# A start-up and a schedule changed at once: load order, word conversion, warm-up length and the order of the late products in a fused attention and expert kernel

## The chip, the cores and the metric

The kernel runs on one core of one Trainium2 chip. The metric is the device time of one execution in microseconds (us), the smaller the better.

## The reference

The reference is an attention block whose keys and queries go through a polynomial sketch, followed by four experts. It is cut here to what the argument needs.

```python
def _attn_ref(q, k, v, S1, S2):            # q, k, v: (4, 4, 1088, 32), S1 and S2: (8, 32)
    def phi(x):
        a = np.einsum('rd,bhsd->bhsr', S1, x)
        b = np.einsum('rd,bhsd->bhsr', S2, x)
        return np.einsum('bhsi,bhsj->bhsij', a, b).reshape(*x.shape[:-1], r * r)
    q_p, k_p = phi(q), phi(k)
    kv = np.einsum('bhsf,bhsd->bhfd', k_p, v)
    z = np.sum(k_p, axis=2)
    num = np.einsum('bhsf,bhfd->bhsd', q_p, kv)
    den = np.einsum('bhsf,bhf->bhs', q_p, z)[..., None] + 1e-06
    return num / den
# ... x is the attention's output, 4352 tokens by 128; then for four experts
#     out += p[:, e] * (relu(x @ w1[e]) @ w2[e])        # w1: 128 x 1024, w2: 1024 x 128
```

S1 and S2 arrive as 64-bit floats. The kernel reads them as pairs of 32-bit words and makes 32-bit floats of them with integer operations.

## The kernel before

Nothing can be projected until S and the first batch of k are on the chip. The start-up therefore is a race: S's two loads, word operations on VectorE and a transpose on one side, k's load and its transpose on the other. TensorE meanwhile runs matmuls on zeros to get its clock up: in the profile below the full clock is granted from 4.33.

```python
s_raw = cpool.tile([R2, 2 * D], I32, name="s_raw")
for i, (eng, src) in enumerate(((nc.scalar, S1), (nc.sync, S2))):
    eng.dma_start(s_raw[R * i : R * i + R, :], src.bitcast(I32))
# ...
load_rows(k, 0, "kn")                     # 128 rows of 4352 bytes, on SyncE
load_rows(q, 0, "qn", slice(0, P))
vn[0] = load_v(0)
# ...
keep_warm(10)                             # 128x128x512 bf16 matmuls on zeros
# ...
bits(s_f[:, hi], high, 1, shl, 21, shr)   # first of 14 word operations
# ...
nc.vector.tensor_tensor(out=s_hl[0:R2, :], in0=s_n[:, :], in1=s_f[:, :].bitcast(F32), op=ALU.mult)
nc.vector.transpose(s_T[:, :], s_hl[:, :])
for h in range(H):                        # weights of the key projection
    nc.scalar.copy(_ap(sk, ...), _ap(s_T, ...))
for i in range(3):
    nc.gpsimd.tensor_copy(_ap(sp, ...), _ap(s_T, ...))
for h in range(H):                        # weights of the query projection
    nc.gpsimd.tensor_copy(_ap(sr, ...), _ap(sp, ...))
# ...
def start():                              # in this order: transposes of k and q, key projection (h<-sk,kT),
    ...                                   # query projection (o<-qT,sr), sums over keys (f<-vx,kp),
                                          # den and num of the first 128 tokens, division, first expert
```

The later units of tokens are cut into pieces that are dealt out between the expert matmuls. `yield` ends a piece; the schedule counts 19 pieces a unit. A late piece is the product of queries with the summed keys (den<-kvx,qp on TensorE), which needs two products made by VectorE, p = 0 and p = 1.

```python
            for p in range(2):
                query_product(qp, p, x, n, qa, qb)
                yield
        yield
        yield
        yield from (attend_first if b == 0 and c < START[2] else attend)(b, c, n, qp)
# ... in attend():
            for t in range(T[0]):
                for p in range(2):
                    for _ in range(2):
                        on_side(...)      # one den<-kvx,qp matmul
# ... in attend_first():
        nc.vector.transpose(dT[:, 0:n], nd[0][:, 0:n])
        nc.vector.tensor_scalar(out=rc, in0=_ap(dT, ...), scalar1=1e-6, ...)   # den + 1e-6
        nc.vector.reciprocal(rc, rc)
```

## Time and profile before

| quantity | before |
|---|---|
| time, median of 4 runs | 491.62 us (491.28 to 491.96) |
| span of the profiled run, granted clock | 489.5 us, 0.999 |
| S landed, k landed | 2.37, 4.94 us |
| first key matmul | 5.82 us |
| clock granted in full from | 4.33 us |
| first expert matmul, last matmul starts | 14.16, 485.88 us |

The table's first line has one run more than the three that the prediction speaks of.

### The profile page before, as it was taken

How to read it: one execution, taken by the hardware profiler on the slowest of the kernel's cores; microseconds unless marked ns; L12 is line 12 of the kernel's file. 1: busy time of each engine (PE TensorE's matmuls, PEld its weight loads, DVE VectorE, ACT ScalarE, POOL GpSimd, SP SyncE). 2: the span in 40 equal slices, each digit the busy share in tenths (PEclk: the TensorE clock that was granted, in tenths of full speed). 3: DMA queues.
4: the chain of work that ended last, by engine and by line, in shares of the span. 5: the costliest groups of instructions: out<-in, count | busy, mean ns of one | idle time of the engine just before them, and what ended most of it. 6: DMA issues, size and time to landing. Idle time of an engine off the chain costs nothing.

```text
span 489.5 us, 11439 instructions
## 1 busy us (share of the span) xinstructions
PE 482.6 (99%) x4602; PEld 361.1 (74%) x4602; DVE 318.5 (65%) x746; ACT 244.4 (50%) x487; POOL 226.8 (46%) x260
## 2 busy tenths in 40 slices
PE   8999999999999999999999999999999999999997
PEld 5877777777767777555777777777777777878997
DVE  6759585868676757768675564575575666665642
ACT  3344463455445634535455464445455455566651
POOL 6052473516355444334555353444555355555570
PEclk9999999999999999999999999999999999999999
DMA  7990230040102520041102200031101200120000
GB/s 207 290 284 22 88 95 1 2 137 1 34 2 80 139 55 1 1 118 23 33 2 87 50 0 1 2 87 23 33 1 55 49 1 1 50 50 2 15 3 18
DMA packets 37588, 26.25 MB, mean 54 GB/s; under 512 B 26016, under 2 KB 34592, under 8 KB 37024
## 3 DMA queue, kind: packets, MB, share of 16 engines
q1 hardware_dynamic: 37520, 25.53, 19.0%
q8 instruction: 36, 0.59, 0.5%
q14 instruction: 16, 0.13, 0.1%
q10 hardware_dynamic: 16, 0.00, 0.0%
HBM read 21.28 MB, written 4.24 MB: 52 GB/s over the span
## 4 chain that ended last, share of the span: by engine, by line
PE 96%; DVE 2%; DMA 1%; issue 0%; ACT 0%; SPq 0%; DVEq 0%
PE h L188 49%; PE o L188 40%; PE f L188 4%; PE den L188 3%; DMA kn<-in_k_dram 1%; DVE qp L450 1%; DVE hid L698 1%; PE num L188 1%; PE h L176 0%; DVE kT L314 0%; ACT hid L723 0%; DVE qa L584 0%; ACT sh L842 0%; SPq L119 0%; DVE xT L486 0%
## 5 line engine op out<-in xcount | busy, mean ns | idle before, releaser
L188 PE MATMUL h<-xT,w_sb 128*64 128x512 f32 (+4 forms) x1408 | 300.2, 495 | 0.5 <-DVE xT L486 0.5
L698 DVE SCALAR_TENSOR_TENSOR hid<-h,hid 128x256 f32<-128x256 f32 (+6 forms) x432 | 203.6, 472 | 148.2 <-ACT hid L723 139.2
L723 ACT ACTIVATE hid<-h 128x512 f32<-128x512 f32 (+3 forms) x288 | 158.4, 550 | 195.0 <-PE h L188 157.0
L188 PE MATMUL o<-hid,w2s 128*64 128x256 f32 (+3 forms) x1152 | 221.6, 355 | 0.0
L188 PE MATMUL o<-hid,w_sb 128*64 128x256 f32 (+3 forms) x864 | 183.9, 355 | 0.0
L188 PEld LDWEIGHTS h<-xT,w_sb 128*64 128x64 f32 x1408 | 144.2, 137 | 51.8 <-issue 9.2
L188 PEld LDWEIGHTS o<-hid,w2s 128*64 128x64 f32 x1152 | 131.7, 137 | 30.9 <-issue 0.2
L838 POOL TENSOR_TENSOR ev<-yz,sh 64x256 f32<-64x256 f32 (+3 forms) x72 | 48.4, 672 | 163.5 <-ACT sh L841 160.8
L188 PEld LDWEIGHTS o<-hid,w_sb 128*64 128x64 f32 x864 | 101.0, 137 | 24.5 <-issue 6.3
L826 POOL TENSOR_TENSOR yz<-ev 128x512 f32<-128x512 f32 (+3 forms) x36 | 42.1, 1170 | 61.8 <-ACT ev L829 61.8
L838 POOL TENSOR_TENSOR ct<-ev 128x512 f32<-128x512 f32 (+3 forms) x36 | 42.0, 1167 | 2.8
L838 POOL TENSOR_TENSOR ct<-ct,gate 128x512 f32<-128x512 f32 (+3 forms) x27 | 32.1, 1189 | 2.1
L838 POOL TENSOR_TENSOR total<-total,ct 128x512 f32<-128x512 f32 (+3 forms) x27 | 31.8, 1179 | 2.1
L450 DVE TENSOR_TENSOR qp<-qa,qb 64x384 f32<-64x384 f32 (+3 forms) x44 | 32.1, 729 | 1.0
L828 ACT COPY ev<-o 128x512 f32<-128x512 f32 (+3 forms) x36 | 19.4, 539 | 11.3 <-PE o L188 10.8
L188 PE MATMUL o<-w_sb,hid 128*64 128x128 f32 x256 | 21.7, 273 | 0.0
L829 ACT COPY ev<-o 128x512 f32<-128x512 f32 (+3 forms) x36 | 19.4, 539 | 2.6
L715 ACT ACTIVATE hid<-h 128x256 f32<-128x256 f32 x24 | 9.2, 384 | 21.2 <-PE h L188 20.7
L188 PEld LDWEIGHTS o<-w_sb,hid 128*64 128x64 f32 x256 | 17.8, 137 | 2.1 <-issue 1.9
L353 DVE TENSOR_TENSOR kp<-fs 128x256 f32<-128x256 f32 (+1 forms) x24 | 14.7, 617 | 0.0
L841 ACT COPY sh<-yz 64x256 f32<-64x256 f32 (+3 forms) x36 | 13.7, 379 | 1.7 <-POOL yz L826 0.8
L842 ACT COPY sh<-yz 64x256 f32<-64x256 f32 (+3 forms) x36 | 13.7, 380 | 0.9
(113 smaller groups left out, 230.2 us busy)
## 6 DMA issues: line engine op xcount, KB each, us to landing
w_sb<-in_moe_w_dram SPq DMA_DIRECT2D x8, 512.0 KB, 7.5
gate<-gates SPq DMA_DIRECT2D x4, 1024.0 KB, 5.5
kn<-in_k_dram SPq DMA_DIRECT2D x4, 544.0 KB, 4.6
vn<-in_v_dram SPq DMA_DIRECT2D x16, 128.0 KB, 4.2
gate<-gates SPq DMA_DIRECT2D x2, 896.0 KB, 5.7
qn<-in_q_dram SPq DMA_DIRECT2D x3, 544.0 KB, 5.5
xd<-y SPq DMA_DIRECT2D x26, 48.0 KB, 1.7
out_dram<-ob SPq DMA_DIRECT2D x16, 64.0 KB, 2.0
```

The source lines that it names most:

```text
L188: nc.tensor.matmul(out(s), weights(s), moving(s), **flags)
L353: eng.tensor_tensor(out=_ap(kps[b], 0, P, 256 * t0 + P * p + 64 * x, [[256, n], [32, 2], [R, 4], [1, R]]), in0=_ap(src, 0, P, off + 4 * x, ...
L450: nc.vector.tensor_tensor(out=qp[p][64 * x : 64 * x + 64, 0:n], in0=qa[64 * p : 64 * p + 64, 0:n], in1=qb[64 * p : 64 * p + 64, 0:n], op=A ...
L698: nc.vector.scalar_tensor_tensor(out=out, in0=src, scalar=0.0, in1=in1, op0=ALU.max, op1=ALU.subtract)
L715: nc.scalar.activation(hd[:, 0 : 2 * n], hp[:, 0 : 2 * n], ACTF.Relu)
L723: nc.scalar.activation(hd[:, n * j : n * j + n], hp[:, 0:n], ACTF.Relu)
L826: add = lambda out, in0, in1, op=ALU.add: nc.gpsimd.tensor_tensor(out=out, in0=in0, in1=in1, op=op)
L828: nc.scalar.copy(_ap(ev, 0, P, 0, [[2 * w, 2], [1, w]]), _ap(a0, 0, P, 0, two))
L829: nc.scalar.copy(_ap(ev, 0, P, w, [[2 * w, 2], [1, w]]), _ap(a1, 0, P, 0, two))
L838: add = lambda out, in0, in1, op=ALU.add: nc.gpsimd.tensor_tensor(out=out, in0=in0, in1=in1, op=op)
L841: nc.scalar.copy(sh[HP:P, 0:w], yz[0:HP, 0, 0:w])
L842: nc.scalar.copy(sh[0:HP, 0:w], yz[HP:P, 1, 0:w])
```

## The change

The intent is to start the real work sooner and to remove a wait in the middle. k's load goes first in SyncE's queue, and both S loads go into ScalarE's. The words take 12 operations instead of 14. The copies of S are shared by ScalarE and GpSimd. The warm-up loses two matmuls. The 1e-6 of the first unit's denominator is added by matmuls. The late products run pair by pair (all tokens of p = 0, then all of p = 1), and a unit gets a 20th, empty piece before them.

```diff
     s_raw = cpool.tile([R2, 2 * D], I32, name="s_raw")
-    for i, (eng, src) in enumerate(((nc.scalar, S1), (nc.sync, S2))):
-        eng.dma_start(s_raw[R * i : R * i + R, :], src.bitcast(I32))
+    load_rows(k, 0, "kn")
+    for i, src in enumerate((S1, S2)):
+        nc.scalar.dma_start(s_raw[R * i : R * i + R, :], src.bitcast(I32))
...
-    load_rows(k, 0, "kn")
     load_rows(q, 0, "qn", slice(0, P))
...
-    keep_warm(10)
+    keep_warm(8)
...
-    def either(out, a, b):
-        nc.vector.tensor_tensor(out=out, in0=a, in1=b, op=ALU.bitwise_or)
+    def either(out, in0, s1, op0, in1):
+        nc.vector.scalar_tensor_tensor(out=out, in0=in0, scalar=s1, in1=in1, op0=op0, op1=ALU.bitwise_or)
...
-    bits(s_x[:, lo], low, 29, shr)
-    either(s_x[:, hi], s_x[:, hi], s_x[:, lo])
+    either(s_x[:, hi], low, 29, shr, s_x[:, hi])
-    bits(s_e[:, :], s_f[:, :], 23, shl)
-    either(s_f[:, :], s_e[:, :], s_m[:, :])
+    either(s_f[:, :], s_f[:, :], 23, shl, s_m[:, :])
...
+    def copy_on(scalar):
+        return nc.scalar.copy if scalar else nc.gpsimd.tensor_copy
     for h in range(H):
-        nc.scalar.copy(...)                      # sk
+        copy_on(h < 2)(...)                      # sk: two on ScalarE, two on GpSimd
...                                              # sp and sr are shared out likewise
         nd = [psum(ps_n, "den"), psum(ps_n, "num")]
+        if c == 0:
+            for _ in range(2):
+                on_side(...eps..., start=True, stop=False)      # den starts from 1e-6
...
-        nc.vector.tensor_scalar(... scalar1=1e-6 ...)
+        if c:
+            nc.vector.tensor_scalar(... scalar1=1e-6 ...)
...
-            for t in range(T[0]):
-                for p in range(2):
+            for p in range(2):
+                for t in range(T[0]):
...
+        yield
         yield
         yield
         yield from (attend_first if b == 0 and c < START[2] else attend)(b, c, n, qp)
...
-            count, columns = count + 19, columns + n
+            count, columns = count + 20, columns + n
```

More of the change, by code (lines that the diff above doesn't have):

```diff
@@ L170 @@
         nc.gpsimd.memset(own2[32 * h : 32 * h + 32, h % 2 : h % 2 + 1], 1.0)
+    eps = cpool.tile([P, 1], F32, name="eps")
+    nc.gpsimd.memset(eps[:, :], 0.0)
+    nc.gpsimd.memset(eps[0:1, :], 1e-6)
     def keep_warm(n):
@@ L214 @@
     bits(s_m[:, lo], high, 31, shr, 31, shl)
+    bits(s_x[:, hi], high, 12, shl, 9, shr)
     bits(s_e[:, hi], s_f[:, hi], float(127 - 1023), ALU.add, 0.0, ALU.max)
     bits(s_e[:, lo], s_f[:, hi], float(127 - 1023 - 52), ALU.add, 0.0, ALU.max)
-    bits(s_x[:, hi], high, 12, shl, 9, shr)
-    bits(s_x[:, lo], low, 29, shr)
-    bits(s_n[:, hi], s_e[:, hi], 1.0, ALU.min)
+    either(s_x[:, hi], low, 29, shr, s_x[:, hi])
     bits(s_n[:, lo], low, 3, shl, 3, shr)
     bits(s_f[:, :], s_e[:, :], 255.0, ALU.min)
-    either(s_x[:, hi], s_x[:, hi], s_x[:, lo])
-    bits(s_e[:, :], s_f[:, :], 23, shl)
-    either(s_m[:, hi], s_x[:, hi], s_m[:, lo])
-    either(s_f[:, :], s_e[:, :], s_m[:, :])
+    either(s_m[:, hi], s_m[:, lo], 0, shl, s_x[:, hi])
+    bits(s_n[:, hi], s_e[:, hi], 1.0, ALU.min)
+    either(s_f[:, :], s_f[:, :], 23, shl, s_m[:, :])
     nc.vector.tensor_tensor(out=s_hl[0:R2, :], in0=s_n[:, :], in1=s_f[:, :].bitcast(F32), op=ALU.mult)
     nc.vector.transpose(s_T[:, :], s_hl[:, :])
+    def copy_on(scalar):
+        return nc.scalar.copy if scalar else nc.gpsimd.tensor_copy
     for h in range(H):
-        nc.scalar.copy(_ap(sk, 32 * h, 32, R2 * h, [[HP, 2], [1, R2]]), _ap(s_T, 0, 32, 0, [[D, 2], [1, R2]]))
+        copy_on(h < 2)(_ap(sk, 32 * h, 32, R2 * h, [[HP, 2], [1, R2]]), _ap(s_T, 0, 32, 0, [[D, 2], [1, R2]]))
     for i in range(3):
-        nc.gpsimd.tensor_copy(
+        copy_on(i == 2)(
             _ap(sp, 0, 32, HP * i, [[32, 2], [R, 4], [1, R]]),
@@ L240 @@
     for h in range(H):
-        nc.gpsimd.tensor_copy(
-            _ap(sr, 32 * h, 32, 32 * h, [[P, 6], [1, 32]]), _ap(sp, 0, 32, 0, [[32, 6], [1, 32]])
-        )
+        copy_on(h > 1)(_ap(sr, 32 * h, 32, 32 * h, [[P, 6], [1, 32]]), _ap(sp, 0, 32, 0, [[32, 6], [1, 32]]))
     mask_lo = [R2 + l % R2 for l in range(32)]
@@ L460, in attend_first @@
         nd = [psum(ps_n, "den"), psum(ps_n, "num")]
+        if c == 0:
+            for _ in range(2):
+                on_side(
+                    lambda s: nd[0][half[s], 0:n],
+                    lambda s: _ap(vx, 0, P, D, [[0, HP]]),
+                    lambda s: _ap(eps, 0, P, 0, [[0, n]]),
+                    start=True,
+                    stop=False,
+                )
         for i in range(2):
@@ L466, in attend_first @@
                     lambda s: qp[s][:, 0:n],
-                    start=True,
+                    start=(i > 0 or c > 0),
                     stop=True,
@@ L474, in attend_first @@
         rc = apool.tile([P, QW // 32], F32, tag="rc", name="rc")
-        nc.vector.tensor_scalar(
-            out=rc[:, 0 : n // 32], in0=_ap(dT, 0, P, 0, [[32, n // 32]]), scalar1=1e-6, scalar2=1.0, op0=ALU.add, op1=ALU.mult
-        )
-        nc.vector.reciprocal(rc[:, 0 : n // 32], rc[:, 0 : n // 32])
+        column = _ap(dT, 0, P, 0, [[32, n // 32]])
+        if c:
+            nc.vector.tensor_scalar(
+                out=rc[:, 0 : n // 32], in0=column, scalar1=1e-6, scalar2=1.0, op0=ALU.add, op1=ALU.mult
+            )
+            column = rc[:, 0 : n // 32]
+        nc.vector.reciprocal(rc[:, 0 : n // 32], column)
         rb = apool.tile([P, UNITS[0][1]], F32, tag="rb", name="rb")
```

## The prediction

In the recorded text below, passages that no trace or run of this case shows are cut, and the cuts are marked: most of one paragraph, and parts of rivals (a) and (c). That k fills the 16 DMA engines is in the trace of before: from 2.4 to 4.2 us they were busy for 94 % of the time.

> **What bounds the kernel now.** I read the page's busy shares first, then TensorE's waits, then the chain of waits and the timeline of the first 17 us.
>
> ```profile
> span 489.5 us, 11439 instructions
> PE 482.6 (99%) x4602; PEld 361.1 (74%) x4602; DVE 318.5 (65%) x746; ACT 244.4 (50%) x487; POOL 226.8 (46%) x260
> ```
>
> TensorE is busy 482.6 of 489.5 us, so only 6.9 us of the span are not matmul time. The wait table of TensorE says where they lie:
>
> ```profile
> PE h L176 <- DVE s_hl L212: 1.2, 1, 1.2
> PE h L188 <- DVE kT L314: 0.8, 1, 0.8
> PE den L188 <- DVE qp L450: 0.6, 1, 0.6
> PE h L188 <- DVE xT L486: 0.5, 1, 0.5
> PE den L188 <- DVE kvz L376: 0.5, 1, 0.5
> ```
>
> Columns: who waited for whom, us in total, times, longest. These five make 3.6 us. The last matmul ends near 486.15 us (timeline of the end), so 3.35 us are the closing output; 3.6 + 3.35 = 6.95, the whole of it. The matmuls that do the work are not touched by the change. What can move is the start-up before the first expert matmul at 14.16 us and the single 0.6 us wait in mid-kernel. The timeline of the start (start, us, engine, line, operation):
>
> ```profile
> 0.74 0.58 ACTq L119 DMA_DIRECT2D s_raw<-in_S_dram  x1
> 1.21 0.37 SPq L93 DMA_DIRECT2D kn<-in_k_dram  x1
> 2.47 0.17 DVE L200 TENSOR_SCALAR s_f<-s_raw 16x32 int32<-16x32 int32 x1 [1.27 <-DMA s_raw<-in_S_dram]
> 4.21 0.23 DVE L228 STREAM_TRANSPOSE s_T<-s_hl 32x64 f32<-32x64 f32 x1
> 4.54 0.90 ACT L234 COPY sk<-s_T 32x32 f32<-32x32 f32 x4 [1.69 <-DVE s_T L228]
> 4.96 1.30 DVE L314 STREAM_TRANSPOSE kT<-kn 128x512 f32<-128x512 f32 x2 [0.52 <-DMA kn<-in_k_dram]
> 5.82 2.32 PE L188 MATMUL h<-sk,kT 128*64 128x64 f32 x72 [0.76 <-DVE kT L314]
> ```
>
> The reader should see two inputs racing to VectorE. S lands at 2.37, its words take 2.47 to 4.44; k lands at 4.94 and VectorE had stood still for 0.52 us. So today k sets the first transpose (4.96), that one lasts 0.71 us, and TensorE starts 0.14 us after its end. From 5.82 to 11.57 TensorE does not stop (2.32 + 0.88 + 0.44 + 2.12 in the chain of waits), and then a VectorE chain comes:
>
> ```profile
> 12.49 0.32 DVE L472 STREAM_TRANSPOSE dT<-den 128x128 f32<-128x128 f32 x1 [0.35 <-PE den L188]
> 12.85 0.17 DVE L475 TENSOR_SCALAR rc<-dT 128x4 f32<-128x4 f32 x1
> 13.05 0.18 DVE L478 RECIPROCAL rc<-rc 128x4 f32<-128x4 f32 x1
> 13.26 0.31 DVE L480 STREAM_TRANSPOSE rb<-rc 128x128 f32<-128x128 f32 x1
> 13.68 0.38 DVE L486 TENSOR_TENSOR xT<-num,rb 128x128 f32<-128x128 f32 x1
> ```
>
> The chain of waits names the four warm-up matmuls (12.60 to 13.64) as xT's releaser. In the built program xT waits for the num matmuls and rb only, so I take that as a coincidence of times: shortening this chain counts. The mid-kernel wait:
>
> ```profile
> 198.61 1.27 POOL L826 TENSOR_TENSOR yz<-ev 128x512 f32<-128x512 f32 x1 [1.57 <-ACT ev L829]
> 198.66 1.63 DVE L450 TENSOR_TENSOR qp<-qa,qb 64x384 f32<-64x384 f32 x1
> 199.21 0.54 PE L188 MATMUL den<-kvx,qp 128*64 128x66 f32 x4
> 200.35 0.80 PE L188 MATMUL den<-kvx,qp 128*64 128x66 f32 x20 [0.61 <-DVE qp L450]
> ```
>
> The last product of a unit took 1.63 us where the median of its group is 0.58, beside a GpSimd add, and TensorE had already come to the products by token: 4 of 24 records ran, then it stood for 0.61 us.
>
> [...] Here the warm-up's weight loads come 0.43 us apart up to 4.16, then close up, and the granted clock is full from 4.33[...].
>
> **The change part by part.** I compared the built orders of both kernels on each engine.
>
> Loads. k is issued at 0.74 instead of 1.21, so it should land at 4.94 - 0.47 = 4.47. S1 stays at 0.74 in ScalarE's queue; S2 now follows it there, at about 0.74 + 0.58 + 0.04 = 1.36. A load of S took 1.46 us (ScalarE) and 1.63 us (SyncE) from issue to landing, so S2 would land at 2.8 to 3.0 alone. But k's packets fill all 16 engines from about 1.72, and they took 0.17 us (median) to 0.92 us each; one such packet ahead makes it 3.0 to 3.9. I take 3.15, so the words start at 3.25 (0.1 after the landing as before).
>
> Words. Fourteen operations and a transpose took 2.47 to 4.44, 1.97 us. Independent ones follow each other by 0.09 us, dependent ones by their 0.17 to 0.21 plus 0.03. Laying the twelve new ones out with those gives the transpose's end 1.67 us after the start: 0.30 saved. So s_T is ready at 3.25 + 1.67 = 4.92, against 4.44 today. That is later than k's new landing (4.47): **the race changes its winner**, S now sets the first transpose, at 4.95 against 4.96. The word operations saved and the earlier k are thus mostly eaten by S2's later load. I put the first matmul's move at -0.1 us, with -0.45 (S2 lands by 2.8) to +0.5 (by 3.7) around it. The lean to the early side is a choice, since the 0.92 us packets are few.
>
> Copies of S. Four sk copies of 0.216 us on ScalarE become two there and two on GpSimd (0.24 each, from the sq copies). With the transpose right behind s_T, four in a row would end 1.0 us after it, later than the 0.04 + 0.71 + 0.14 = 0.89 us to the first matmul; two end after 0.55. So the split costs nothing and keeps them off the path. sr was ready at 6.62 for use at 7.94: hidden already, gain 0.
>
> Warm-up. Two matmuls fewer, in time that TensorE spends waiting: 0.
>
> 1e-6 for the first unit. Two matmuls more (4 records, some 0.06 us each after the fill), put before those that wait for kvz; the 0.46 us of idle there hold them. The tensor_scalar leaves the chain: 13.05 - 12.85 = 0.20 us, all on the path. The reciprocal stays. Gain 0.2.
>
> Products by token. I replayed the schedule of pieces. A unit has 20 pieces instead of 19, one of them empty between last product and TensorE's use. For the unit at 200 us the distance grows from 2 work calls to 3 (one call is about 1.6 us of TensorE time), and pair by pair the first 12 of the 24 records need the other product only. Either covers 0.61 us. The smallest distance left is 2, for the unit near 75 us, and the pair order gives it 0.4 us more. Expected gain 0.6 times 0.85 = 0.5.
>
> Sum: -0.1 - 0.2 - 0.5 = -0.8; with the later loads a little earlier as well, I say -0.9: 491.6 - 0.9 = **490.7 us**.
>
> **Rivals.** (a) S2 stuck behind k. For it: [...]k's packets on every engine. [...] A landing at 3.9 would make the first matmul some 0.7 us later and leave the whole near 491.4. (b) The first expert's weights become the wait: the trace's landings show 15 of 16 parts of the first w1 by 12.19 and the last at 13.55, and SyncE's issues from 4.95 on hardly move (one of them waits for k). TensorE will ask at about 13.85, so it holds unless the start gains over 0.5 us; it caps the gain there. (c) The clock: [...] the key projection runs at half rate, 1 to 2 us lost. Against: the change came at 4.33 with the eighth just begun, and the three runs of before agree within 0.36 us. (d) A new wait elsewhere, because all pieces shift: one more meeting of product and GpSimd add would give the 0.6 back, 491.2.
>
> **Range and chances.** The terms span 490.0 (S2 early, wait gone) to 491.5 (S2 late, wait back); runs scatter by 0.2. Eight in ten: 490.1 to 491.4. Two per cent is 9.8 us, more than all the idle time TensorE has, so faster by that is excluded by the 6.9 us; slower would need a stall that nothing here shows.
>
> **What would show it.** k's landing near 4.5, S2's between 2.8 and 3.9, s_T's transpose without a wait for k behind it; first key matmul within 0.5 us of 5.8; the reciprocal directly behind dT and xT some 0.2 us sooner after den; no den wait for qp near 200 us; TensorE's busy time unchanged within 1 us. I am wrong if TensorE waits for a w1 or xT load, if a new wait of over 0.5 us turns up after 20 us, or if the clock is granted after 5 us.

## More of the kernel before

The page's view by stretches gives each engine's busy time with the number of instructions, then the mean granted clock of TensorE. This is the stretch in which the key projection lies:

```profile
core 0: us, PE busy (x) PEld busy (x) DVE busy (x) ACT busy (x) POOL busy (x), PEclk, DMA share, GB/s
5.00:10.00 5.00, 4.24 (x123) 4.21 (x124) 3.64 (x12) 2.67 (x9) 3.71 (x10) 1.00 0.90 206
```

TensorE gets 123 matmuls done in these 5 us, at a granted clock of 1.00.

## The result and the profile after

The changed kernel is correct and took 495.08 us in the median of four runs (494.45 to 495.78) against 491.62. The ratio is 1.0071, with an interval from 1.0053 to 1.0088: 0.7 % slower, inside the 2 % band but outside the predicted range, on the wrong side.

The page's span and busy shares after:

```profile
span 493.2 us, 11440 instructions
PE 484.6 (98%) x4604; PEld 371.6 (75%) x4604; DVE 317.2 (64%) x743; ACT 245.0 (50%) x488; POOL 227.2 (46%) x261
```

Two things grew: TensorE's busy time by 2.0 us with only two records more, and what is not busy time from 6.9 to 8.6 us. Busy time that grows at equal work means matmuls that ran slower; the 72 key matmuls alone took 3.87 us instead of 2.32, as the timeline below shows. TensorE's waits:

```profile
PE h L193 <- DVE kT L319: 2.7, 1, 2.7
...
PE h L193 <- DVE hid L716: 0.5, 1, 0.5
PE h L193 <- PE h L181: 0.3, 1, 0.3
PE den L193 <- DVE kvz L381: 0.2, 1, 0.2
```

The wait for qp near 200 us is gone from the table, as predicted. The wait for the first transpose went from 0.8 to 2.7 us, and a wait for hid is new. The timeline of the start, in the columns that the prediction explains:

```profile
0.74 0.90 ACTq L120 DMA_DIRECT2D s_raw<-in_S_dram  x2
...
4.86 0.17 DVE L205 TENSOR_SCALAR s_f<-s_raw 16x32 int32<-16x32 int32 x1 [3.66 <-DMA s_raw<-in_S_dram]
6.28 0.23 DVE L232 STREAM_TRANSPOSE s_T<-s_hl 32x64 f32<-32x64 f32 x1
6.45 1.25 DVE L319 STREAM_TRANSPOSE kT<-kn 128x512 f32<-128x512 f32 x2
7.25 3.87 PE L193 MATMUL h<-sk,kT 128*64 128x64 f32 x72 [2.73 <-DVE kT L319]
...
14.99 0.44 PE L193 MATMUL den<-qp,kvz 128*64 128x128 f32 x4 [0.24 <-DVE kvz L381]
...
15.48 0.32 DVE L486 STREAM_TRANSPOSE dT<-den 128x128 f32<-128x128 f32 x1 [0.34 <-PE den L193]
15.83 0.18 DVE L495 RECIPROCAL rc<-dT 128x4 f32<-128x4 f32 x1
```

The words start at 4.86 instead of 2.47, because S landed at 4.76. k had landed at 4.43. The 72 key matmuls not only start 1.43 us later, they also last 3.87 us instead of 2.32. The stretches say why:

```profile
5.00:10.00 5.00, 2.75 (x56) 2.78 (x58) 3.48 (x19) 2.27 (x7) 1.90 (x7) 0.75 0.81 183
10.00:15.00 5.00, 4.76 (x124) 4.51 (x121) 3.12 (x13) 1.46 (x5) 3.50 (x13) 0.91 1.06 359
```

The granted clock is 0.75 and 0.91 where it was 1.00. The trace's clock events put it at full rate from 4.12, at half rate from 7.53 to 10.95 (3.41 us), then at full rate again. The sum, all from starts in the two timelines:

| step | before | after | moved by |
|---|---|---|---|
| first key matmul | 5.82 | 7.25 | +1.43 |
| key projection, until the query projection starts | 2.12 long | 3.64 long | +1.52 |
| query projection to den<-qp,kvz | 4.07 long | 4.10 long | +0.03 |
| den<-qp,kvz to first expert matmul | 2.15 long | 1.95 long | -0.20 |
| first expert matmul | 14.16 | 16.94 | +2.78 |
| first expert matmul to the start of the last matmul | 471.72 long | 472.46 long | +0.74 |

So two questions have to be answered: why S2 came so late, and why the clock fell back. The 0.74 us of the middle is a third, smaller one.

### The profile page after: what moved, and what is told of

Read it like the earlier page. It is cut to its first block, busy times and chain, and to the rows that moved or that the text cites. A ratio compares the mean times of both kernels' runs of the same rounds, so it can differ in the third digit from the quotient of the medians.

```text
span 493.2 us, 11440 instructions
## 1 busy us (share of the span) xinstructions
PE 484.6 (98%) x4604; PEld 371.6 (75%) x4604; DVE 317.2 (64%) x743; ACT 245.0 (50%) x488; POOL 227.2 (46%) x261
## 4 chain that ended last, share of the span: by engine, by line
PE 94%; DVE 2%; issue 1%; DMA 1%; POOL 1%; ACT 0%; ACTq 0%; DVEq 0%; POOLq 0%
PE h L193 49%; PE o L193 39%; PE f L193 3%; PE den L193 3%; DVE hid L716 1%; DMA s_raw<-in_S_dram 1%; DVE kp L358 1%; PE num L193 0%; ACT hid L741 0%; PE h L181 0%; POOL sq L676 0%; POOL kp L358 0%; DVE kT L319 0%; ACT fs L351 0%; ACTq L120 0%
## 5 line engine op out<-in xcount | busy, mean ns | idle before, releaser
L193 PEld LDWEIGHTS h<-xT,w_sb 128*64 128x64 f32 x1408 | 148.3, 137 | 49.5 <-issue 6.6
L455 DVE TENSOR_TENSOR qp<-qa,qb 64x384 f32<-64x384 f32 (+3 forms) x44 | 30.7, 697 | 1.2
```

The source lines that it names most:

```text
L193: nc.tensor.matmul(out(s), weights(s), moving(s), **flags)
L455: nc.vector.tensor_tensor(out=qp[p][64 * x : 64 * x + 64, 0:n], in0=qa[64 * p : 64 * p + 64, 0:n], in1=qb[64 * p : 64 * p + 64, 0:n], op=A ...
```

## The experiments

My theory after the result: S2, now issued at 1.35 us behind S1, stood behind all of k's data on the DMA engines, and that gap of idle TensorE cost the clock its full rate. The main rival: the late S explains only part, and the shorter warm-up loses the clock by itself. A second rival, for the rest: the new pieces cost something. Eleven kernels were run; all gave correct results. Eight were built to take the change apart or to alter one cause, two repeat a kernel, and one is an attempt at a better version. The kernel before ran beside them on the same chip, with medians of 491.48 to 491.58 us.

### The old load order in the changed kernel (u_loads)

```diff
-    load_rows(k, 0, "kn")
-    for i, src in enumerate((S1, S2)):
-        nc.scalar.dma_start(s_raw[R * i : R * i + R, :], src.bitcast(I32))
+    for i, (eng, src) in enumerate(((nc.scalar, S1), (nc.sync, S2))):
+        eng.dma_start(s_raw[R * i : R * i + R, :], src.bitcast(I32))
...
+    load_rows(k, 0, "kn")
     load_rows(q, 0, "qn", slice(0, P))
```

> The changed kernel with the load order of before put back (S1 on ScalarE's queue, S2 first and k second on SyncE's), all else as changed, eight warm-up matmuls too. Theory (S2's load behind k costs the start, and the clock falls because TensorE then stands still for 2.7 us): S lands at 2.4, the words end at about 4.1, k lands at 4.9, the first key matmul comes at about 5.8 instead of 7.25, the clock is granted throughout from about 4.2 on, time 495.1 - 1.4 - 1.5 = about 492.1 us. Rival (two warm-up matmuls fewer are what loses the clock): first key matmul at 5.8, but the clock still falls for 3.4 us near 7.5, about 493.6. Rival (the loss lies in mid-kernel, not in the start): above 494.

Measured: 492.81 us (491.05 to 492.88), ratio 1.0018 (1.0006 to 1.0031). Two lines of its start:

```profile
2.39 0.17 DVE L205 TENSOR_SCALAR s_f<-s_raw 16x32 int32<-16x32 int32 x1 [1.19 <-DMA s_raw<-in_S_dram]
...
6.09 3.81 PE L193 MATMUL h<-sk,kT 128*64 128x64 f32 x72 [1.30 <-DVE kT L319]
```

The words are back at 2.39 and the first key matmul at 6.09, so 2.3 of the 3.5 us went with the loads. But the key matmuls still took 3.81 us: in this run the clock was granted for the first time at 9.41. Four of the five runs lie at 492.6 to 492.9 and one at 491.05. The late S is not the whole cause.

### The new load order alone in the kernel before (b_loads)

```diff
-    for i, (eng, src) in enumerate(((nc.scalar, S1), (nc.sync, S2))):
-        eng.dma_start(s_raw[R * i : R * i + R, :], src.bitcast(I32))
+    load_rows(k, 0, "kn")
+    for i, src in enumerate((S1, S2)):
+        nc.scalar.dma_start(s_raw[R * i : R * i + R, :], src.bitcast(I32))
...
-    load_rows(k, 0, "kn")
```

> The kernel before with the new load order alone (k first on SyncE's queue, S1 and S2 on ScalarE's); fourteen word operations, ten warm-up matmuls. Theory: S2 lands at about 4.8, the words end 0.3 us later than in the changed kernel, first key matmul at about 7.5, TensorE still for 2.5 us after the ten warm-up matmuls, the clock falls for one 3.4 us window in most runs: 491.6 + 1.7 + 1.5 = about 494.8 us. Rival (the ten warm-up matmuls hold the clock): 493.3, no fall of the clock. Rival (loads are hidden): 491.6.

The 3.4 us of this text are the half-rate stretch in the changed kernel's profile, 7.53 to 10.95.

Measured: 495.27 us (495.09 to 495.79), ratio 1.0078 (1.0064 to 1.0092). The load order alone costs as much as the whole change. The words started at 4.88, the clock ran at half rate from 7.55 to 10.96 (3.41 us), and the key projection waited for something else than the transpose:

```profile
7.95 3.67 PE L188 MATMUL h<-sk,kT 128*64 128x64 f32 x72 [2.99 <-ACT sk L234]
```

Here four sk copies in a row on ScalarE end at 7.85 us, after the transpose. The changed kernel, with the same late S, started at 7.25: the shorter words and the shared copies together are worth 0.70 us, once S is what is waited for.

### More warm-up in the changed kernel (u_warm18)

```diff
-    keep_warm(8)
+    keep_warm(18)
```

> The changed kernel with 18 warm-up matmuls instead of 8, so that TensorE works until about 6.7 and not 4.5; first key matmul unchanged near 7.25. Theory (the still stand loses the clock): granted throughout, the key projection takes 2.3 us instead of 3.9, time 495.1 - 1.5 = about 493.6 us. Rival (the projection is slow for another reason, data or contention): no gain, 495. If the warm-up is still running when k is ready, the gain is smaller.

Measured: 493.11 us (492.32 to 493.68), ratio 1.0032 (1.0018 to 1.0045). The start, and the stretch of the key projection:

```profile
7.55 2.32 PE L193 MATMUL h<-sk,kT 128*64 128x64 f32 x72 [0.55 <-DVE kT L319]
```
```profile
5.00:10.00 5.00, 4.45 (x88) 3.16 (x87) 3.85 (x19) 2.60 (x9) 2.23 (x8) 1.00 0.77 180
```

With ten matmuls on zeros more, the clock stays full through the gap (granted at 4.77 and kept) and the key projection is back at 2.32 us, although it starts later than in the changed kernel's own profile. That gains 1.97 us on the changed kernel's first four runs, and 1.23 on its repeat below. What is left, 1.6 us over before, is the late S2 with the rest of the change; that rest is worth nothing measurable by itself, as u_loads_w10 below shows.

### Fewer warm-up matmuls in the kernel before (b_warm8)

```diff
-    keep_warm(10)
+    keep_warm(8)
```

> The kernel before with 8 warm-up matmuls instead of 10 and nothing else: first key matmul unchanged at 5.8, TensorE still from 4.6 to 5.8 (1.2 us) instead of 5.05 to 5.8. Theory (the two matmuls count, as the runs with the load order put back suggest, in which 4 of 5 took 492.8 and one 491.05): most runs lose part of the clock, 1 to 2 us, a few don't; median near 493. Rival (warm-up count is harmless while the still stand is short): 491.5 like before.

Measured in six runs: 493.11 us (491.69 to 495.10), ratio 1.0032 (1.0016 to 1.0049). The profiled run, which was the slowest of them:

```profile
7.06 4.11 PE L188 MATMUL h<-sk,kT 128*64 128x64 f32 x72 [2.26 <-DVE kT L314]
```

Two matmuls on zeros, which TensorE had run in time that it spent waiting, are worth 1.6 us in the median. In the profiled run the clock was granted for the first time at 12.66. k's landing was late in that run as well, at 5.93, so its 495.10 is not the clock alone.

### k's load in two halves (u_k2parts)

```diff
-    load_rows(k, 0, "kn")
+    load_rows(k, 0, "kn", slice(0, S // 2))
+    load_rows(k, 0, "kn", slice(S // 2, S))
     for i, src in enumerate((S1, S2)):
```

> The changed kernel with k's load in two parts of half the columns, both ahead on SyncE's queue. Theory (an engine drains what one load has given it, here 8 records, before it takes ScalarE's queue): S2's packets start after the first half of k, near 2.9 instead of 3.7, S2 lands at 3.5 to 4.0 instead of 4.76, first key matmul at about 6.3, time 0.9 to 1.5 us below the changed kernel (493.6 to 494.2; the clock will still fall in most runs). Rival (S2 waits for all of k's bytes, whatever the parts): packets at 3.7, landing 4.7, 495.

Measured: 493.19 us (491.52 to 493.57), ratio 1.0025 (1.0012 to 1.0037).

```profile
3.74 0.17 DVE L206 TENSOR_SCALAR s_f<-s_raw 16x32 int32<-16x32 int32 x1 [2.54 <-DMA s_raw<-in_S_dram]
```

The trace's DMA records settle the queueing. In the changed kernel k's 128 records of 4352 bytes, eight for each of the 16 engines in the mean, started at 1.78 to 3.81, and S2's eight records of 256 bytes came at 3.70 to 3.96. When the first of them started, 121 of k's 128 had. With k cut into two loads, S2's came at 2.84 to 3.15, while k's second half still ran until 3.75. When S2's first record started, 127 of the 256 records of the halves had. So in these two runs S2 waited for nearly all the records of the load that was being served, 128 in each, not for one record and not for everything that was queued. The two alone cannot tell a whole load from a count of eight records an engine. The trace of best_split, below, speaks against the count: there the part of k on SyncE's queue is 512 records of 512 bytes, 32 for each engine in the mean, and ScalarE's part, issued 0.16 us behind it, had its first record at 3.24, when 288 had started, 18 for each engine. (SyncE's part took 1.09 us from issue to first record; by that estimate ScalarE's could have begun at 2.45.) The records do not name their engine, so that each engine finished its 32 first is not shown. S landed at 3.64, and the first key matmul was at 6.13. The time was 1.2 us below that of the changed kernel's repeat in the same rounds (494.34), as expected. It was still 1.7 us above the kernel before, though the first key matmul was only 0.3 us later: the clock came only at 9.08.

### Pair order and 20 pieces in the kernel before (b_pairs20), and pair order alone (b_pairs)

```diff
-            for t in range(T[0]):
-                for p in range(2):
+            for p in range(2):
+                for t in range(T[0]):
 ...                                       # the next lines in b_pairs20 only
+        yield
 ...
-            count, columns = count + 19, columns + n
+            count, columns = count + 20, columns + n
```

> The kernel before with the products by token pair by pair and 20 pieces a unit alone; start untouched (first key matmul 5.8, first expert matmul 14.2). Theory A (the stalls in mid-kernel follow from where the pieces stand): the stall at 200 us is gone (-0.75 us), and small ones like those of the changed kernel near 75 us and 135 us appear (+0.4 and +1.0): about 492.3 us. Theory B (stalls are chance meetings of VectorE and GpSimd, moved by the later start): the stall at 200 us gone and none new, about 490.9. The distance tells them apart only with the profile: each stall has a place.

> The kernel before with the products by token pair by pair, 19 pieces as before: for the places of the stalls in the profile alone. Theory: the stall near 200 us shrinks from 0.75 us to 0.3 us or nothing, as 12 of the 24 records need the earlier product only, and the new stall near 78 us (sums of keys waiting for their products) does not come, since it follows from the 20 pieces. Rival (pair order brings it): it is there.

Measured: with 20 pieces 491.45 us (491.31 to 491.85), ratio 1.0001 (0.9988 to 1.0013). With pair order alone one run of 491.53 us, of unknown state, beside a median before of 491.58. Neither moves the time measurably. The timelines show why. With the pair order and 20 pieces the stall near 200 us is gone, but the sums over keys (f<-vx,kp) near 76 us have to wait for VectorE's key products. In the kernel before, the last of those was this:

```profile
73.23 0.52 DVE L353 TENSOR_TENSOR kp<-fs 128x320 f32<-128x320 f32 x1
```

With 20 pieces:

```profile
72.20 1.13 DVE L353 TENSOR_TENSOR kp<-fs 128x320 f32<-128x320 f32 x1
74.21 1.57 DVE L353 TENSOR_TENSOR kp<-fs 128x320 f32<-128x320 f32 x2
...
76.41 0.22 PE L188 MATMUL f<-vx,kp 128*64 128x66 f32 x1
```

Two products start at 74.21 and together take 1.57 us, and the last of the sums starts at 76.41, where it was at 75.0 before (0.6 of this is the later start of that profile). The waits of TensorE's matmuls do not list this stall; those of its weight loads have 0.4 us of it. An estimate from the starts of all its records, the time that passed less what their columns take at the usual pace, gives some 0.7 us lost between 60 and 80 us, about what was won at 200. Pair order alone leaves 76 us as it was, and only shrinks the stall at 200:

```profile
199.59 0.77 PE L188 MATMUL den<-kvx,qp 128*64 128x66 f32 x12
200.74 0.57 PE L188 MATMUL den<-kvx,qp 128*64 128x66 f32 x12 [0.38 <-DVE qp L450]
```

Twelve records run while the last product is made, and 0.38 us of waiting remain of 0.61. So the pair order does what it is meant to; the 20th piece shifts other pieces into a new meeting.

### The changed kernel again (r_after)

The kernel is the changed one without an edit.

> The changed kernel once more, on the chip of the other experiments. Expected as on record, 494.4 to 495.8; [...] the theory wants the key projection to be cold, in whole or for the greater part, in nearly all runs, since TensorE is still from 4.5 to 7.3 us in each. A profile with a fully granted projection and a time near 493.3 would speak for it too; one with a fully granted projection and a time of 495 against it.

Measured in six runs: 494.34 us (492.68 to 496.17), ratio 1.0047 (1.0035 to 1.0059). The slowdown holds on another occasion, and its size varies. In the profiled run of 496.17 us the clock was granted for the first time at 12.84. The stated mean clock of that run is 1.0 nevertheless, as it is of the stretches of u_loads before its first grant: a start that is cold from the beginning does not show in the mean.

### Old loads and ten warm-up matmuls in the changed kernel (u_loads_w10, and again r_loads_w10)

```diff
-    keep_warm(8)
+    keep_warm(10)
 ...                                       # and the load order of before, as in u_loads
```

> The changed kernel with the load order of before and with ten warm-up matmuls: what is left of the change is the shorter word chain, the shared copies, the 1e-6 in the first unit and the products pair by pair with 20 pieces. Theory: the loss is all in the loads and the warm-up, so this one is no slower than before and gains 0.2 us (1e-6) plus some 0.3 us (mid-kernel): about 491.0. Rival (some of the loss is in the other parts): 491.5 or above.

> The changed kernel with the old load order and ten warm-up matmuls again, to narrow its interval (0.9979 to 1.0003 of the kernel before so far). Theory: 0.2 to 0.5 us below before, 491.0 to 491.3. If it comes out at before's time or above, the rest of the change is worth nothing measurable.

Measured: 491.22 us (490.93 to 491.46), ratio 0.9991 (0.9979 to 1.0003), and in the repeat 491.93 us (491.61 to 492.52), ratio 1.0010 (0.9996 to 1.0023). Both intervals hold 1. With the two costly parts undone, the slowdown is gone, and what remains of the change gains nothing that these runs can tell from zero. From the first profile:

```profile
6.03 2.32 PE L193 MATMUL h<-sk,kT 128*64 128x64 f32 x72 [0.38 <-DVE kT L319]
```

k landed at 5.14 there and at 5.44 in the repeat, against 4.94 in the profile of before. With the old order k is the later input, so the words that finish sooner wait for it. From den<-qp,kvz to the first expert matmul it took 1.95 us instead of 2.15: the 0.20 of the removed operation is there.

### k split in the order of need (best_split)

This was the version that the experiments pointed to: S first on both queues, then the columns of the first transpose behind S2 on SyncE, and the rest of k behind S1 on ScalarE, with ten warm-up matmuls.

```diff
 ...                                       # S loads as before, keep_warm(10)
-    load_rows(k, 0, "kn")
 ...
+    kn[0] = lpool.tile([P, S], F32, tag="kn", bufs=2, name="kn")
+    for eng, c0, steps in ((nc.sync, 0, [[8 * D, 4], [1, P]]), (nc.scalar, P, [[8 * D, 4], [1, P]]), (nc.scalar, 8 * P, [[1, 2 * D]])):
+        eng.dma_start(_ap(kn[0], 0, P, c0, steps), bass.AP(k.tensor, k.offset + c0, [[G * D, P]] + steps))
```

> The changed kernel with S1 and S2 each first in its own queue as before, ten warm-up matmuls, and k's load in the parts that the transposes need: the columns of the first behind S2 on SyncE's queue, those of the second and the last 64 behind S1 on ScalarE's. Theory: the first part is half the bytes, so it lands near 4.2 instead of 4.9 to 5.2 (the start of the records and 512-byte pieces permitting), the words end at 3.9 to 4.1, so the first key matmul comes at about 5.2 instead of 5.8 to 6.0: 0.5 to 0.7 us below the same kernel with k whole, about 490.6. Rival: the parts share the engines and 512-byte pieces are slow, the first part lands near 5 as well: 491.2.

On the 512-byte pieces of the rival: in the first 5.2 us of the trace of before a record of 512 bytes took 27 ns in the median (19 bytes a ns) and one of 4352 bytes 168 ns (26 bytes a ns).

Measured: 492.52 us (491.60 to 492.83), ratio 1.0015 (1.0003 to 1.0028). The first part landed at 4.43 and the first key matmul came at 5.31, about half a microsecond sooner than before, as hoped. But from there to den<-qp,kvz it took 6.93 us instead of 6.19, because ScalarE waited 1.48 us for v's load (0.39 before) and the copies and products that the sums over keys need came later behind it, and the first expert matmul was at 14.19, no sooner than before. It beats neither the kernel before nor the version with old loads and ten warm-up matmuls. Why most of its timed runs were about 1 us slower than the profiled one of 491.60 was not settled.

## Why the prediction was wrong, and where it was right

**The step that failed first is the landing of S2.** The prediction had the right mechanism in its hands, as its rival (a), and mis-sized it: "one such packet ahead makes it 3.0 to 3.9. I take 3.15". S2 landed at 4.76. I took it that one 4352-byte record of k, 0.17 to 0.92 us in the trace of before, would go ahead of S2's records. No trace had shown that: in the one of before, S's last record (1.98) starts before k's first (2.20). In the changed kernel 121 of k's 128 records had started before S2's first. The halved k is the experiment on it: 2.84 instead of 3.70 for S2's first record, with 127 of the 256 records of the halves started. A second, smaller error lies behind it: S2's records began at 3.70 to 3.96, but the landing followed 0.8 us after the last of them instead of the 0.4 us of the kernel before. Why it did was not shown. Consequence: -0.1 us was predicted for the first key matmul, and +1.43 was measured.

**The step that failed second is the warm-up.** The prediction says "Two matmuls fewer, in time that TensorE spends waiting: 0", and calls rival (c) unlikely because three runs of before agree. Those runs had ten warm-up matmuls and a short gap behind them; they could not speak for eight. The profiles show what the two were worth. The eight run without a gap from 1.19 to 4.79 when the clock is not granted, and these 3.6 us were not enough in four of the five profiles that have eight: the first grant came at 9.41 (u_loads), 12.66 (b_warm8), 9.08 (u_k2parts) and 12.84 (r_after), and the key projection took 3.64 to 4.11 us. Only in the changed kernel's own profile did they get it, at 4.12. In the seven profiles with ten, the projection took 2.32 us in five and 2.68 in b_pairs20; only b_loads, whose S2 came late, took 3.67.

For why eight were enough once and four times not, there is an estimate only. The changed kernel's clock events lie 3.41 us apart (4.12, 7.53, 10.95), and the half-rate stretch of b_loads lasts 3.41 us too. So I looked at how busy TensorE was in the 3.41 us that end at a change of the clock. Before a first grant it was busy for 86 % (after), 92 % (before), 89 % (b_pairs20) and 99.6 % (u_loads_w10, 2.24 to 5.66); before a loss for 20 % (after, 4.12 to 7.53) and 24 % (b_loads). In the 3.41 us after the grant of the kernel before it was busy for 78 %, and the clock was kept. Laid back by another 3.41 us or two from the first grant, stretches that no grant followed were busy for 65 % (u_loads), 70 and 64 % (b_warm8), 74 % (u_k2parts), 64 and 48 % (r_after) and 66 % (b_pairs20). That such stretches follow one another from the start is taken from the three events of the changed kernel, not shown for the others. Ten matmuls last longer (to 5.64 in u_loads_w10, with the first key matmul at 6.03) and nearly join the key projection. Ten did not always suffice either, but lost less: in the profile of b_pairs20 the clock came at 6.86, within the projection, which took 2.68 us instead of 2.32. In the changed kernel's own profile the eight were enough to get the clock, and the gap from 4.52 to 7.25, made by S2, lost it. In its repeat they were not enough.

The two costs can be read from timed medians. The late S2 with the clock kept is 1.6 us (u_warm18). The clock on top is 1.2 to 2.0 us (the changed kernel's two sets of runs less u_warm18). The parts are not simply additive, since a longer gap and a shorter warm-up slow the same matmuls (the key projection took 3.67 us in b_loads, 4.11 in b_warm8 and 3.87 in the changed kernel, against 2.32): the new loads alone cost 3.8 us, the shorter warm-up alone 1.6.

**Half right: the middle.** The 0.6 us at 200 us went: the pair order alone left 0.38 of it (b_pairs), and with the extra piece as well nothing was left (b_pairs20). The extra piece alone was not run. The prediction's rival (d), a new wait that takes the place, is what happened: a stall of some 0.7 us near 78 us, which b_pairs20 shows and b_pairs does not, so it comes with the 20th piece. The replay of the schedule looked only at the distance between a unit's last product and its use, and not at the key products. A second new wait, for hid near 138 us (0.5 and 0.4 us), appears in the changed kernel's two profiles. It is absent from all other profiles with 20 pieces, u_warm18 among them, which has all of the change and a start 1.25 us earlier. Those have their first expert matmul by 15.73 us, the two with the wait at 16.94 and 18.25. The kernel b_warm8, with 19 pieces and a start at 18.00, does not have it either. So it goes with 20 pieces and a late start together; its cause stays open.

**Right: the rest of the start.** The words and their transpose took 1.65 us instead of 1.97, with 0.30 predicted. The tensor_scalar's 0.20 on the path was gained to the hundredth. The 1e-6 matmuls fitted in the idle time before kvz, whose wait fell from 0.5 to 0.2. The shared copies stayed off the path, and b_loads shows what four in a row would have done. The load of the first expert's weights never became the wait: TensorE's release at 16.94 was not a load. The change of winner of the race was right too, only far bigger than thought. "TensorE's busy time unchanged within 1 us" failed, with +2.0, and was the plainest sign of the clock.

**The range** failed since its late end, 491.4, took S2's worst case as 3.9 and gave the clock no share, though it stood among the rivals with 1 to 2 us.

## What to carry to other kernels

A small load that everything waits for goes ahead of a big one in time, also when another engine's queue would carry it: here S2, on ScalarE's queue, landed at 4.76 us behind k and S at 2.37 ahead of it. If that cannot be, try to cut the big load: with k in two halves S landed at 3.64. Warm-up is not idle filling: with eight matmuls and the old loads the clock came at 9.41, with eighteen and the new loads it was full from 4.77 and stayed so up to the first real matmul at 7.55. So lengthen the warm-up when a change delays that matmul, and time a start-up several times, because the first grant differs from run to run (4.12 us in one profile of the changed kernel, 12.84 in the other). Moving the pieces of a schedule away from one stall can move others into a new one, so compare the lag along the whole run and not at the stall alone.
